# Engine programs in the main program instead of in a block, in a kernel of windowed attention and a gated spatial mixer

## The chip, the cores and the metric

One core of one Trainium2 chip runs the kernel. The metric is device time in microseconds (us). A run gives one such time. One further execution was taken by the hardware profiler; its span runs from the program's first recorded instruction to the end of its last.

## What is computed

`x` is 2048 rows of 512 values, bfloat16. It is normalised once, and two branches read the result; their sum and `x` are the output.

```python
xn = _layernorm(x)
# A: attention, 32 heads of 16, each row looks at 8 rows, 2 apart, up to itself
qkv = xn @ wqkv
logits = einsum('bhsd,bhswd->bhsw', q, kg) * scale     # kg, vg: gathered windows
o = einsum('bhsw,bhswd->bhsd', softmax(logits), vg)
# B: gated mixer, Fh = 896
z = gelu(xn @ w_in); z1 = z[..., :Fh]; z2 = _layernorm(z[..., Fh:])
g = einsum('ts,bsf->btf', w_sp, z2) + b_sp[None, :, None]
return x + o @ wo + (z1 * g) @ w_out
```

## The kernel before

The 2048 rows are 16 blocks of 128 (loops over `b`) and four groups of 512 (loops over `j` and `tc`). `ln_block` normalises a block on DVE, with the power on POOL (L561), and transposes it on PE (L573) or by DMA. `v_block` makes V (L598), which ACT evicts and POOL writes to a scratch tensor in DRAM (L606), from which SP later reads shifted windows (L846). `qk_pair` makes Q and K (L615), `prods` multiplies and adds windows on DVE (L636, L641), PE reduces over the head's 16 values (L649), `softmax` is DVE and ACT work. `z2_block` and `z1_group` make the two halves of z (L696, L740); `g_group` is the large product with `w_sp` (L823); `pv_block` weighs V by the attention on DVE (L851 to L857); `out_block` multiplies with `wo` (L879) and `w_out` (L888), DVE adds `x` (L894), and SP stores 128 rows (L899). The last block of rows is split by columns, and its second part is stored by ACT's queue.

None of this is issued where it is written. Every operation is a task in a `Plan`: an engine, a function that issues it, an estimated duration, what it reads and writes. `schedule` orders the tasks of each engine on a modelled clock. `emit` then goes over the engines in the order PE, ACT, DVE, POOL, SP and, for each, issues its tasks in its order; ahead of a task stand waits on semaphores (L310) for those tasks of other engines that it needs and that no earlier wait has covered. A DMA has a semaphore of its own channel.

The change touches how these five lists become programs. `build_kernel` opens `nc.Block()` (L391) within `with ExitStack() as es:` (L387). `emit` gets it as `block`, and `starters` (L283) maps an engine to `block.tensor`, `block.scalar`, `block.vector`, `block.gpsimd` or `block.sync`. Each of these opens a stretch of program for its engine, runs `body` in it, puts a jump into that stretch in the main program, and a jump to a common end behind it. When the `ExitStack` closes, the block writes the common end: each engine drains its own pipeline (DRAIN) and then meets the others: the engines count up a semaphore, POOL waits until all have, and then releases them all (EVENT_SEMAPHORE). The profile gives what the block adds at its end to L387.

What is written before that belongs to the launch (L952): small constants set by POOL, and a meeting of the same form, which every engine passes ahead of its first task.

The last thing in SP's list is `sp_final` (L927), the plan's final hook: it waits (L929) until the semaphores of all channels that write to DRAM, the scratch tensor's and the output's, have their full count.

Of the kernel before, what the change touches and what calls it, by code (L numbers as in the profile page):

```python
# [36 lines left out]
class Plan:  # L37
# [213 lines left out]
                                                                     last / 1000.0))  # L251


    def emit(self, nc, block, sems, chan_sems):
        for t in self.tasks:
            for d in t.deps:
                d.used = True
        cnt = {e: 0 for e in ENGS}
        for e in ENGS:
            for t in self.order[e]:  # L260
                if t.dma is None and t.used:
                    cnt[e] += 1
                    t.count = cnt[e]
                    t.tok = (("E", e), t.count)
        ccnt = {}
        for t in self.tasks:
            if t.dma is not None:
                c = t.dma["chan"]
                ccnt[c] = ccnt.get(c, 0) + 16
                t.count = ccnt[c]  # L270
                t.tok = (("C", c), t.count)
        self.chan_totals = dict(ccnt)
        for t in sorted(self.tasks, key=lambda x: (x.start, x.idx)):
            ck = {}
            for d in t.deps:
                for k, v in d.clock.items():
                    if ck.get(k, 0) < v:
                        ck[k] = v
            if t.tok is not None:
                ck[t.tok[0]] = max(ck.get(t.tok[0], 0), t.tok[1])  # L280
            t.clock = ck

        starters = {"pe": block.tensor, "act": block.scalar, "dve": block.vector, "pool": block.gpsimd,  # L283
                    "sp": block.sync}

        def semof(key):
            return sems[key[1]] if key[0] == "E" else chan_sems[key[1]]

        def run_engine(e):
            def body(eng):  # L290
                known = {}
                for t in self.order[e]:
                    need = {}
                    dl = [d for d in t.deps if known.get(d.tok[0], 0) < d.tok[1]]
                    for d in dl:
                        k, v = d.tok
                        implied = False
                        for d2 in dl:
                            if d2 is d:
                                continue  # L300
                            c2 = d2.clock.get(k, 0)
                            if c2 > v or (c2 == v and d2.tok != d.tok):
                                implied = True
                                break
                        if implied:
                            continue
                        if need.get(k, 0) < v:
                            need[k] = v
                    for k, v in need.items():
                        eng.wait_ge(semof(k), v)  # L310
                    for d in t.deps:
                        for k, v in d.clock.items():
                            if known.get(k, 0) < v:
                                known[k] = v
                    last = t.fn(eng)
                    assert last is not None, "task %s returned no instruction" % t.name
                    if t.dma is not None:
                        last.then_inc(chan_sems[t.dma["chan"]], 16)
                    elif t.used:
                        last.then_inc(sems[e], 1)  # L320
                fh = getattr(self, "final_hooks", {}).get(e)
                if fh:
                    fh(eng)
            starters[e](body)

        for e in ENGS:
            run_engine(e)


def build_kernel(nc, A_x, A_wqkv, A_wo, B_x, B_w_in, B_w_sp, B_b_sp, B_w_out, out, report=False, emit=True):  # L330
# [54 lines left out]
    plan = Plan()  # L385

    with ExitStack() as es:  # L387
        ar = es.enter_context(nc.sbuf_tensor("arena", [128, AR], BF))
        fp = es.enter_context(nc.sbuf_tensor("fpool", [128, FR], F32))
        ps = es.enter_context(nc.psum_tensor("ps", [128, PR], F32))  # L390
        block = es.enter_context(nc.Block())  # L391
        sem_h = {e: es.enter_context(nc.semaphore("sem_" + e)) for e in ENGS if e != "sp"}

        def A(name, n, o2_=0):
# [529 lines left out]
        chan_sems = {c: es.enter_context(nc.semaphore("c_%d" % i)) for i, c in enumerate(chans)}  # L924
# [4 lines left out]
                eng.wait_ge(chan_sems[c], plan.chan_totals[c])  # L929
        plan.final_hooks = {"sp": sp_final}  # L930
        with nc.allow_low_precision("bf16 intermediates by design"):
            plan.emit(nc, block, sem_h, chan_sems)
    return plan

def bass_parallel_sum__sliding_local_dilated__mixer_gmlp__prompt_kernel(
    nc, A_x, A_wqkv, A_wo, B_x, B_w_in, B_w_sp, B_b_sp, B_w_out, out
):
    build_kernel(nc, A_x, A_wqkv, A_wo, B_x, B_w_in, B_w_sp, B_b_sp, B_w_out, out)
# [28 lines left out]
```

## Time and profile before

| | |
|---|---|
| runs | 240.87, 241.27, 241.40 us; median 241.27 |
| the profiled execution's own time | 242.69 us |
| its span | 239.3 us (239.34 with one more digit); 3.35 us of its time lie outside |
| granted TensorE clock, mean | 0.999 |
| PE busy | 234.0 us, 98% of the span |
| DVE busy | 212.8 us, 89% |
| ACT, POOL busy | 98.1 and 33.2 us |
| PE rows on the chain that ended last | 69% of the span |

The span holds the launch's opening part and everything that the kernel writes, up to the last instruction of the block's common end. What the chip does before and after that in the measured time shows in no row. Lines with a "q" after the engine's name are of the engine's sequencer: waits, jumps, drains, issues of DMAs; they count for no busy time. In the answers about one line, the three numbers are the shortest, median and longest duration in nanoseconds, and behind them stand the starts of the first and the last one in us from the start of the span. A semaphore instruction that waits shows its whole wait as its duration on SP's queue in some rows (1965 ns for the longest at L929), and only its own few nanoseconds in others.

### The profile page before, as it was taken

What the parts mean: (1) busy time and instruction counts of PE and PEld (TensorE: products, weight loads), DVE (VectorE), ACT (ScalarE), POOL (GpSimd) and SP (SyncE); (2) the same over time, 40 slices, a digit from 0 to 9 for tenths busy, and PEclk for the clock granted to TensorE, in tenths of its full rate; (3) what the DMA queues carried; (4) which work ended last, traced back from release to release, by engine and by line L of the source; (5) the groups of instructions that cost most, each with busy time, mean ns of one, the idle gap of its engine ahead of it and who ended that gap; (6) DMA issues with size and microseconds to landing.
All of it is one profiled execution on the core that took longest, in us unless ns stands there. A gap on an engine that the chain in (4) does not pass through costs nothing.

```text
span 239.3 us, 3165 instructions
## 1 busy us (share of the span) xinstructions
PE 234.0 (98%) x1212; PEld 112.7 (47%) x1233; DVE 212.8 (89%) x267; ACT 98.1 (41%) x144; POOL 33.2 (14%) x56
## 2 busy tenths in 40 slices
PE   7999999999999999999999999999999999999995
PEld 3555555555444444444454444444444444444444
DVE  3798889999989899999999999986898999999952
ACT  2596889899888975541112111001010100101100
POOL 2378350401383500000000000000000000000000
PEclk9999999999999999999999999999999999999999
DMA  5997969993327110004079999999999997942112
GB/s 185 364 316 145 224 151 215 208 208 76 114 108 244 62 37 10 0 8 170 0 228 320 182 245 258 267 168 294 309 344 244 282 325 244 271 141 55 22 44 66
DMA packets 77806, 42.81 MB, mean 179 GB/s; under 512 B 50129, under 2 KB 77153, under 8 KB 77793
## 3 DMA queue, kind: packets, MB, share of 16 engines
q1 hardware_dynamic: 76480, 40.13, 66.2%
q0 software_dynamic: 800, 2.11, 2.8%
q10 hardware_dynamic: 512, 0.38, 0.5%
q8 instruction: 9, 0.15, 0.2%
q14 instruction: 5, 0.03, 0.1%
HBM read 26.35 MB, written 4.21 MB: 128 GB/s over the span
## 4 chain that ended last, share of the span: by engine, by line
PE 69%; DVE 16%; POOL 7%; issue 4%; POOLq 1%; ACT 1%; DVEq 0%
PE ps L823 40%; PE ps L888 10%; PE ps L879 6%; DVE arena L641 5%; PE ps L598 5%; DVE arena L636 4%; PE ps L615 3%; POOL fpool L723 3%; DVE arena L726 2%; PE ps L696 2%; POOL fpool L561 2%; PE ps L541 2%; POOL vscr L606 1%; POOLq L387 1%; DVE arena L563 1%
## 5 line engine op out<-in xcount | busy, mean ns | idle before, releaser
L823 PE MATMUL ps<-arena 128*128 128x512 bf16 x440 | 98.6, 379 | 0.4
L823 PEld LDWEIGHTS ps<-arena 128*128 128x128 bf16 x448 | 43.7, 98 | 52.6
L831 ACT ACTIVATE arena<-ps 128x1024 bf16<-128x1024 f32 (+1 forms) x16 | 14.7, 917 | 104.4 <-PE ps L823 93.8
L636 DVE TENSOR_TENSOR arena<-arena 128x4096 bf16<-128x4096 bf16 x16 | 36.6, 2285 | 0.2
L851 DVE TENSOR_TENSOR arena<-arena 128x4096 bf16<-128x4096 bf16 x16 | 36.5, 2284 | 0.0
L854 DVE TENSOR_TENSOR arena<-arena 128x2048 bf16<-128x2048 bf16 (+1 forms) x32 | 30.5, 953 | 0.4
L615 PE MATMUL ps<-arena 128*128 128x512 bf16 x126 | 28.5, 379 | 0.1
L641 DVE TENSOR_TENSOR arena<-arena 128x4096 bf16<-128x4096 bf16 x12 | 27.5, 2288 | 0.2
L888 PE MATMUL ps<-arena 128*128 128x512 bf16 (+2 forms) x116 | 26.8, 366 | 0.2
L696 PE MATMUL ps<-arena 128*128 128x448 bf16 x128 | 26.0, 352 | 0.0
L740 PE MATMUL ps<-arena 128*128 128x512 bf16 x109 | 24.2, 379 | 0.2
L615 PEld LDWEIGHTS ps<-arena 128*128 128x128 bf16 x128 | 14.5, 113 | 13.0
L894 DVE TENSOR_TENSOR arena<-ps,arena 128x512 bf16<-128x512 f32 (+2 forms) x17 | 11.2, 657 | 9.4 <-PE ps L888 9.4
L624 ACT ACTIVATE arena<-ps 128x1024 bf16<-128x1024 f32 x16 | 16.2, 1019 | 4.3 <-PE ps L615 3.6
L696 PEld LDWEIGHTS ps<-arena 128*128 128x128 bf16 x128 | 12.4, 98 | 11.5
L888 PEld LDWEIGHTS ps<-arena 128*128 128x128 bf16 x119 | 11.6, 98 | 12.7
L740 PEld LDWEIGHTS ps<-arena 128*128 128x128 bf16 x112 | 10.8, 98 | 12.7
L746 ACT ACTIVATE arena<-ps 128x1024 bf16<-128x1024 f32 (+1 forms) x16 | 14.1, 916 | 6.1 <-PE ps L740 6.1
L879 PE MATMUL ps<-arena 128*128 128x512 bf16 (+2 forms) x67 | 16.5, 366 | 0.1
L702 ACT ACTIVATE arena<-ps 128x896 bf16<-128x896 f32 x16 | 14.6, 913 | 2.8 <-PE ps L696 2.6
L598 PE MATMUL ps<-arena 128*128 128x512 bf16 x60 | 14.9, 379 | 0.4 <-ACT arena L579 0.2
L707 ACT ACTIVATE arena<-arena 128x896 bf16<-128x896 bf16 x16 | 15.2, 949 | 0.2
(56 smaller groups left out, 176.4 us busy)
## 6 DMA issues: line engine op xcount, KB each, us to landing
arena<-vscr SPq DMA_DIRECT2D x16, 1024.0 KB, 6.8
arena<-in_A_x_dram SPq DMA_DIRECT2D x29, 128.0 KB, 5.3
vscr<-arena POOLq DMA_DIRECT2D x16, 128.0 KB, 2.8
out_dram<-arena SPq DMA_DIRECT2D x15, 128.0 KB, 5.1
arena<-in_A_wqkv_dram SPq DMA_DIRECT2D x2, 512.0 KB, 6.6
arena<-in_B_w_in_dram SPq DMA_DIRECT2D x2, 448.0 KB, 5.2
arena<-in_B_w_in_dram SPq DMA_DIRECT2D x1, 896.0 KB, 5.3
arena<-in_B_w_out_dram SPq DMA_DIRECT2D x1, 896.0 KB, 5.5
```

The source lines that it names most:

```text
L598: last = t.matmul(P(bk, 512), AC(off["xnT"] + dc * S + 128 * b, [[1, 128]]), AC(off["wv"] + 512 * dc, [[1, 512]]), start=(dc == 0), stop=( ...
L615: last = t.matmul(P(bk, 512, 512 * which), AC(off["wqk"] + 2048 * which + 512 * dc + c, [[4, 128]]), AC(off["xnT"] + dc * S + 512 * j, [[1 ...
L624: T("act", lambda a: a.activation(AC(qo, [[ko - qo, 2], [1, 512]]), P(bk, 1024).rearrange("p (t n) -> p t n", t=2), ACTF.Copy, scale=0.5), ...
L636: T("dve", (lambda pbv, qb, kb: lambda v: v.tensor_tensor(pbv, qb, kb, ALU.mult))(pbv, qb, kb), reads=rd, writes=[("pb", s_)], est=c_tt(40 ...
L641: T("dve", (lambda av, bv: lambda v: v.tensor_tensor(av, av, bv, ALU.add))(av, bv), reads=[("pb", 1)], writes=[("pb", acc)], est=c_tt(4096 ...
L696: last = t.matmul(P(bk, 448, 512 * hf), AC(off["xnT"] + dc * S + 128 * b, [[1, 128]]), AC(off["w_in2"] + 896 * dc + 448 * hf, [[1, 448]]), ...
L740: last = t.matmul(P(bk, 512, 512 * i), AC(off["w_in1"] + 896 * dc + 128 * fc, [[1, 128]]), AC(off["xnT"] + dc * S + 512 * j, [[1, 512]]), ...
L823: last = t.matmul(P(bk, 512, 512 * i), AC(off["z2"] + FH * sh + 128 * fc, [[1, 128]]), AC(off["wT%d" % r_] + sh * 512, [[1, 512]]), start= ...
L851: T("dve", lambda v: v.tensor_tensor(tv, tv, av, ALU.mult), reads=[("attn", b)], writes=[("Vs", sv)], est=c_tt(4096), name="pv%d" % b, pri ...
L854: T("dve", (lambda n: lambda v: v.tensor_tensor(A("Vs", n, 4096 * sv), A("Vs", n, 4096 * sv), A("Vs", n, 4096 * sv + n), ALU.add))(n), wri ...
L879: last = t.matmul(P(bk, cn), AC(off["OT"] + 512 * tb + 128 * cc, [[1, 128]]), AC(off["wo"] + 512 * cc + c0, [[1, cn]]), start=(cc == 0), s ...
L888: last = t.matmul(P(bk, cn), AC(off["z1T"] + fc * S + 128 * tb, [[1, 128]]), AC(off["w_out"] + 512 * fc + c0, [[1, cn]]), start=False, sto ...
```

## The change

`emit` no longer takes a block. Each engine's `body` is called with the engine itself, so that its tasks, its waits and the final hook go into the main program, one engine's after the other's. `nc.Block()` is not opened. Thus the jumps into the engines' stretches, the jumps to the common end, the drains and the meeting at the end are not written. Tasks, their order, waits between them, buffers and DMAs are as before.

```diff
-    def emit(self, nc, block, sems, chan_sems):
+    def emit(self, nc, sems, chan_sems):
...
-        starters = {"pe": block.tensor, "act": block.scalar, "dve": block.vector, "pool": block.gpsimd,
-                    "sp": block.sync}
+        engines = {"pe": nc.tensor, "act": nc.scalar, "dve": nc.vector, "pool": nc.gpsimd, "sp": nc.sync}
...
-            starters[e](body)
+            body(engines[e])
...
-        block = es.enter_context(nc.Block())
...
-            plan.emit(nc, block, sem_h, chan_sems)
+            plan.emit(nc, sem_h, chan_sems)
```

## Prediction, made before the result was known

> **What bounds the kernel now.** I read the page's head first, then the shares of the chain of work that ended last.
>
> ```profile
> span 239.3 us, 3165 instructions
> ...
> PE 234.0 (98%) x1212; PEld 112.7 (47%) x1233; DVE 212.8 (89%) x267; ACT 98.1 (41%) x144; POOL 33.2 (14%) x56
> ...
> PE 69%; DVE 16%; POOL 7%; issue 4%; POOLq 1%; ACT 1%; DVEq 0%
> ```
>
> The reader is to see that the body is PE's, at 98% of the span, and that the rest of the chain is DVE, POOL and issue. The change edits no task, no order and no wait of this body. So the body can only be shifted as a whole, by what happens ahead of the first tasks; what else the change is worth lies behind the last store.
>
> Next I read the answers on the two lines that write sequencer instructions around the body: L952, the launch's opening, and L387, the block's end. First the opening; starts are in us.
>
> ```profile
> L952 SPq EVENT_SEMAPHORE  x1: 17/17/17, 0.7 to 0.7; - x1
> L952 ACTq EVENT_SEMAPHORE  x1: 17/17/17, 0.7 to 0.7; - x1
> L952 DVEq EVENT_SEMAPHORE  x1: 21/21/21, 0.7 to 0.7; - x1
> L952 PEldq EVENT_SEMAPHORE  x1: 51/51/51, 0.7 to 0.7; - x1
> ```
>
> ```profile
> L387 POOLq EVENT_SEMAPHORE  x2: 17/17/17, 239.2 to 239.2; - x2
> L387 POOLq DRAIN  x1: 4537/4537/4537, 80.1 to 80.1; - x1
> L387 PEldq DRAIN  x1: 512/512/512, 236.4 to 236.4; - x1
> L387 DVEq DRAIN  x1: 395/395/395, 236.7 to 236.7; - x1
> L387 ACTq DRAIN  x1: 153/153/153, 237.5 to 237.5; - x1
> L387 SPq COMPARE_BRANCH  x1: 41/41/41, 238.9 to 238.9; - x1
> L387 SPq DRAIN  x1: 13/13/13, 239.1 to 239.1; - x1
> L387 SPq EVENT_SEMAPHORE  x1: 17/17/17, 239.3 to 239.3; - x1
> ...
> L387 PEldq EVENT_SEMAPHORE  x1: 51/51/51, 239.3 to 239.3; - x1
> ```
>
> Two things are to be seen. Of the ten jumps in the source, five in and five out, only one is in the profile, on SP, at the end. And four engines have drained long before the end: POOL by 84.7, PE by 236.9, DVE by 237.1, ACT by 237.7 us. They wait for SP. What SP waits for is in the view of SP's own waits, and the last work in the timeline from 236.4 us on:
>
> ```profile
> SPq L929 <- DMA out_dram<-arena: 2.0, 1, 2.0
> ...
> SPq L387 <- PEq L387: 0.2, 1, 0.2
> ```
>
> ```profile
> 236.73 0.36 DVE L894 TENSOR_TENSOR arena<-ps,arena 128x192 bf16<-128x192 f32 x1 [0.41 <-PE ps L888]
> 237.12 0.36 ACTq L899 DMA_DIRECT2D out_dram<-arena  x1
> ```
>
> ACT issues the last store at 237.12; SP's wait for its landing ends at 238.69 (1.965 us from 236.725). That landing sets the end, and everything after it is SP alone.
>
> **The change part by part.** *SP's end.* After the landing the trace has, on SP: three more waits, starting at 238.737, 238.810 and 238.874, each 28 ns; the COMPARE_BRANCH at 238.941, 41 ns, which also carries SP's last wait (on a channel that landed long before); DRAIN at 239.119; POOL's two semaphore instructions at 239.157 and 239.235; the release on SP at 239.276, and on PE at 239.288 for 51 ns, which is the span's end, 239.339. After the change the last wait still has to be made, as a plain one in place of the branch: 238.941 + 0.028 = 238.969. All that comes later goes. So the span loses 239.339 - 238.969 = 0.37 us, and nothing is late next: the other engines' last rows end at 237.5 or before.
>
> *The drains* cost nothing now and nothing when gone: the one on POOL (4.5 us) lies beside 155 us of idle POOL, and those of PE, DVE and ACT end at least 1.0 us before the landing that SP waits for.
>
> *The jumps into the blocks.* The profile has no row for them. SP's first DMA issues at 0.797, 61 ns after its release from the opening meeting (0.719 + 0.017); between SP's waits at the end the gaps are 36 to 45 ns. The jump that did run was followed by 137 ns (238.982 to 239.119). A jump of that price does not fit into SP's 61 ns, so I take nothing; the upper bound for a hidden gain is 61 ns, were the whole gap the jump's, the lower bound zero, since the gap cannot fall below nothing. ACT's gap is 71 ns, POOL's 103, DVE's 172. POOL's and DVE's don't reach the end: their first tasks (memsets) feed warm-up matmuls and constants, while the first block's normalisation waits for x, whose DMAs SP and ACT issue.
>
> The Trainium skill prices these in "Advanced Engine Details and Errata", section "Control Flow Timing": about 51 ns for an unconditional branch and 108 ns for one that compares. The row at the end shows 41 ns and a gap, and no row shows an unconditional one; by the skill's figure the entry would give another 0.05 us and my time would be 0.05 us lower.
>
> *The part outside the span.* The profiled execution took 242.69 us, and 3.35 us of that lie outside the span, in no row. The engines must leave their programs there and, somehow, be known to have ended. The change can move this part both ways. At one end, the meeting that is removed is waited for again out there: +0.37 us, which gives back all. At the other, the four engines that are through at 237.7 do what they have to do after their programs under SP's wait: at most that wait's length, -1.97 us. Nearest to a small gain are the rows of the meeting itself: its steps from the last arrival on are 78 ns (239.157 to 239.235) and 41 ns (to 239.276), and a meeting to which all but SP have long come saves at most some such steps. I take -0.1 us, about one to two steps, and keep both ends.
>
> "Runtime: NRT & Kernel Launch", section "The ~15µs preamble/postamble breakdown", of the same skill speaks against the change: the runtime puts a barrier of its own, about 1.5 us, behind every kernel, which waits for all engines. No row here shows it. By it the kernel's own meeting is one of two, and what is saved is the first alone, 0.37 us; it gives no more.
>
> *Sum.* Against the profiled execution: 242.69 - 0.37 - 0.10 = 242.22 us, with a span of 238.97. That execution stands 1.42 us above the median of the runs; the same steps from the median give 241.27 - 0.47 = 240.80 us, 0.19% less.
>
> **The rivals.** *Moved, not saved.* The engines must be joined behind the kernel as well; if that join starts with the same drain and the same steps for SP, the span shows 0.37 us less and the part outside 0.37 us more: 241.27 us. For it: nothing in the span shows that the end of the program needs no join. Against: SP would have to pay a second time what it pays now, and the outside part would have to grow.
>
> *Much more than the span.* If the engines have work of their own after their programs, the removed meeting held it back until 239.3 for all of them. Then up to 1.97 us more goes; half of that, about 1.0, as the middle of an unknown, gives 241.27 - 0.37 - 1.0 = 239.9 us. For it: 3.35 us outside is nine times the meeting. Against: SP comes last either way, and its own part stays on the path.
>
> *Slower: an instruction fetch that is no longer covered.* The page has PE's programs coming by DMA:
>
> ```profile
> q8 instruction: 9, 0.15, 0.2%
> ```
>
> Nine transfers of 16 KB; their records last 0.88 to 1.33 us. Now none shows as a stall. The five programs are laid out anew, and where a piece of program begins relative to the 16 KB piece may shift. If one fetch comes to stand open on PE in the stretch from 101 to 236 us, where PE is busy 134.4 of 135 us, its whole 0.88 to 1.33 us reach the end: 240.80 + 0.88 to 240.80 + 1.33, 241.7 to 242.1 us. It decides from the point where more than 0.47 us of a fetch is uncovered, over 0.95 before a measurement can tell it. Against: the instructions between the opening and the last task are the same ones in the same number, and the removed ones are two or three per engine, at the end.
>
> *It does nothing at all*: the end is written in any case. Then no row at L387 would vanish and the time is 241.27; that is as good as excluded by the diff, and it goes with the first rival.
>
> **How the numbers follow.** This kernel's measurement can tell about 0.2%, 0.48 us, so faster begins below 240.79 and slower above 241.75. My forecast, 0.37 us of the span and little outside (240.6 to 241.0), gets 0.57; its point sits on the bound, so 0.32 of that is faster and 0.25 same. Moved, not saved: 0.12, same. Much more than the span: 0.18, faster. An open fetch: 0.11, taken as slower. The last 0.02 is same. That is 0.50 faster, 0.39 same, 0.11 slower. The predicted time is the forecast's, 240.80. The range has to leave out at most 0.2: it leaves the open fetch (0.11) and the lower half of the third case (0.09, below 239.9), so it goes from 239.9 to 241.6; the upper end takes in the case of no gain with the runs' own scatter of up to 0.4 us.
>
> **What would show it.** Right: no DRAIN, jump or semaphore row after SP's four waits at the end; SP's last wait ends near 238.97 and the span is 239.0; the first DMA issues again at 0.80 and the first PE matmul at 1.25; PE's busy time stays at 234.0; the execution's time less its span is 3.2 to 3.4 us. Moved, not saved: that difference rises to 3.7. Much more: it falls below 3.0. Open fetch: a gap on PE of about 1 us with no releaser. Entry jumps, if they did cost: the first DMA issues at 0.74 instead of 0.80. I am wrong at the root if the body itself changes length, by another order of tasks or other waits, since I took it as the same.

## The result, and the profile after

Over 22 executions each, the changed kernel took 240.41 us (239.94 to 242.48) and the kernel before 241.46 us (240.87 to 243.25). The ratio is 0.9965, with a 95% interval of 0.9950 to 0.9981: faster, by some 0.8 us and between 0.5 and 1.2. The medians stand 1.05 us apart, within that interval.

The page of the changed kernel's profiled execution (240.36 us), the lines that answer to those shown of before:

```profile
span 238.8 us, 3154 instructions
...
PE 233.8 (98%) x1212; PEld 112.6 (47%) x1233; DVE 212.8 (89%) x267; ACT 98.1 (41%) x144; POOL 33.2 (14%) x56
...
q8 instruction: 9, 0.15, 0.2%
...
PE 83%; DVE 12%; POOL 3%; issue 1%; ACT 0%; ACTq 0%
```

There are eleven instructions less in all. The engines' counts are the same, and their busy times agree to within 0.25 us. The chain's shares differ (PE 83% and POOL 3%, against 69% and 7%) with no task moved. Most likely the walk back took another of two near releasers in the first 100 us, where several engines lie close together; nothing is concluded from it.

The block's rows are gone from the trace. In their place, the last instructions are SP's waits, now at L927, and the opening (now L950) is as it was:

```profile
L927 SPq EVENT_SEMAPHORE  x5: 17/28/28, 238.5 to 238.8; - x5
```

```profile
L950 SPq EVENT_SEMAPHORE  x1: 17/17/17, 0.7 to 0.7; - x1
L950 ACTq EVENT_SEMAPHORE  x1: 17/17/17, 0.7 to 0.7; - x1
```

SP's first DMA issues at 0.799 us (0.797 before), the first matmul starts at 1.253 (1.251). So the entry gained nothing. At the end, the last store's issue and landing, from the timeline and from SP's waits:

```profile
236.59 0.36 DVE L892 TENSOR_TENSOR arena<-ps,arena 128x192 bf16<-128x192 f32 x1 [0.41 <-PE ps L886]
236.98 0.35 ACTq L897 DMA_DIRECT2D out_dram<-arena  x1
```

```profile
SPq L927 <- DMA out_dram<-arena: 2.0, 1, 2.0
```

The wait for the landing ends at 238.560, four more waits end at 238.832, and that is the span's end: 0.272 us behind the landing, where it was 0.649 (238.690 to 239.339). That is 0.377 us. The other 0.13 us by which this pair of spans differs (239.339 and 238.832, that is 0.507) came from the body, whose last store issued 0.14 us earlier. Bodies scatter: the changed kernel's spans went from 238.3 to 240.9 us. So spans are compared by their medians from here on.

What the single profiled execution of before could not tell is the part outside the span. Each execution of the comparisons has its own span, rounded to 0.1 us, and its own time; but for a few outliers, their difference scatters less than either. For the kernel before, in 31 executions taken together with the first experiments, the difference has a median of 2.22 us (28 of them between 2.16 and 2.26, then 2.34, 3.15 and 3.34). For the changed kernel it is 1.55 us (22 executions, 1.42 to 1.82 and one of 2.41). So 0.67 us went there, more than in the span, and the 3.35 us of the first profile were an exception (7 of 98 executions of before had 2.9 or more, counted over all comparisons of the next section).

### The profile page after: what moved, and what is told of

It reads as the page before. It is cut to its first block, busy times and chain, and to the rows that moved or that the text cites. A ratio compares the mean times of both kernels' runs of the same rounds, so it can differ in the third digit from the quotient of the medians.

```text
span 238.8 us, 3154 instructions
## 1 busy us (share of the span) xinstructions
PE 233.8 (98%) x1212; PEld 112.6 (47%) x1233; DVE 212.8 (89%) x267; ACT 98.1 (41%) x144; POOL 33.2 (14%) x56
## 4 chain that ended last, share of the span: by engine, by line
PE 83%; DVE 12%; POOL 3%; issue 1%; ACT 0%; ACTq 0%
PE ps L821 40%; PE ps L613 11%; PE ps L886 10%; PE ps L694 9%; PE ps L877 6%; DVE arena L639 4%; DVE arena L634 4%; PE ps L596 3%; POOL fpool L721 3%; PE ps L539 2%; DVE arena L724 2%; PE ps L647 1%; DVE arena L662 1%; DVE fpool L659 0%; PE ps L571 0%
```

## The experiments

The theory after the result: the removed meeting cost SP its 0.37 us in the span and held back all engines' ends, and letting these go early shortens the part outside by 0.67 us. The rivals: the jumps and the layout of the blocks cost something that no row shows; an instruction transfer for PE behind the span went (the trace of before has one of 16 KB at 241.70 us, 1.29 us long, the trace after has none there); what counts is SP's own drain and late release, not the others'.

All edits but that of the control are to the changed kernel. "Outside" is time less span; both it and the span are medians over the executions. The runs were made on three chips: e1 to e4, e5 to e8 and e9 to e12. Each ratio is to the kernel before on the same chip, whose part outside has medians of 2.22, 2.21 and 2.20 us there. On the chip of e5 to e8 no kernel ran with all engines let go early, so that the 1.55 us they are set against is from other chips.

| run | ratio to before, 95% interval | time, us | span, us | outside, us |
|---|---|---|---|---|
| before, with the first four | | 241.58 | 239.30 | 2.22 |
| changed (the result) | 0.9965 (0.9950 to 0.9981) | 240.41 | 238.90 | 1.55 |
| e1_before | 0.9998 (0.9982 to 1.0013) | 241.56 | 239.20 | 2.22 |
| e2_meeting | 1.0007 (0.9990 to 1.0024) | 241.77 | 239.45 | 2.21 |
| e3_pe_pad | 0.9951 (0.9929 to 0.9974) | 240.44 | 238.90 | 1.53 |
| e4_last_wait | 0.9938 (0.9913 to 0.9963) | 239.95 | 238.45 | 1.51 |
| e5_hold_all | 0.9979 (0.9969 to 0.9989) | 240.97 | 238.80 | 2.27 |
| e6_hold_pe | 0.9974 (0.9957 to 0.9992) | 240.76 | 238.95 | 1.78 |
| e7_hold_act | 0.9959 (0.9943 to 0.9975) | 240.54 | 238.80 | 1.73 |
| e8_hold_pool | 0.9976 (0.9962 to 0.9989) | 240.98 | 238.95 | 2.03 |
| e9_hold_dve | 0.9959 (0.9946 to 0.9973) | 240.52 | 239.00 | 1.55 |
| e10_act_waits | 0.9956 (0.9939 to 0.9974) | 240.39 | 238.70 | 1.67 |
| e11_pool_waits | 0.9958 (0.9940 to 0.9975) | 240.36 | 238.60 | 1.77 |
| e12_last_wait_again | 0.9949 (0.9930 to 0.9967) | 240.17 | 238.60 | 1.50 |

**The control, e1_before.** No edit.

> The kernel before, unchanged, to learn how much of its time lies outside the span from more than one execution. All theories: ratio 1.00 to within 0.2%, span near 239.4 us. Theory A (the removed meeting and drains are all there is): time less span is about 1.6 us in the usual execution, as in the 22 executions of the changed kernel (1.4 to 1.8, one of 2.4), so that the 3.35 us of the one profiled execution was an exception. Theory B (something behind the span got shorter too): it is 2.0 to 3.4 us in all of them.

Ratio 0.9998. Twelve executions had 2.15 to 2.37 us outside, and one of them 3.07. That settles it: 2.2 us is the rule for this kernel, theory B's lower end, and a reading near 3 us is a thing of single executions. The profiled one of this control had 2.20 us outside and no PE transfer behind its span, so that such a transfer is not what makes the 2.2 us.

**The meeting alone, e2_meeting.**

```diff
             plan.emit(nc, sem_h, chan_sems)
+            nc.all_engine_barrier()
```

> The changed kernel with one all-engine meeting, drains included, written behind the five programs; still no block and no jumps. Theory A: everything comes back, ratio to before 1.000, span as before (about 0.35 us more than changed). Rival J (the jumps and the layout of the blocks cost something that no row shows): the ratio stays near 0.998 or below, since the jumps are still gone.

Everything came back: ratio 1.0007, outside 2.21 us. The answer on the line that writes the meeting has the same rows as the block's end had, less the jump:

```profile
L931 POOLq EVENT_SEMAPHORE  x2: 17/17/17, 239.6 to 239.7; - x2
L931 POOLq DRAIN  x1: 4537/4537/4537, 80.6 to 80.6; - x1
L931 PEldq DRAIN  x1: 513/513/513, 236.9 to 236.9; - x1
L931 DVEq DRAIN  x1: 395/395/395, 237.3 to 237.3; - x1
L931 ACTq DRAIN  x1: 152/152/152, 238.0 to 238.0; - x1
L931 SPq DRAIN  x1: 13/13/13, 239.5 to 239.5; - x1
L931 SPq EVENT_SEMAPHORE  x1: 17/17/17, 239.7 to 239.7; - x1
```

So the blocks' jumps and layout, which are still absent here, were worth nothing that these ratios can tell (the interval is 0.17% to either side, 0.4 us), and the meeting with its drains brings back the saving within that. Its part of the span, from the end of SP's last wait (239.503) to PE's release (239.760), is 0.257 us. The block's end took 0.370, counted from 238.969, where a plain last wait would have ended; the 0.11 us between them are SP's jump with the gap behind it, which the trace shows and the ratio is too coarse to tell.

**PE's instruction transfer, e3_pe_pad.**

```diff
-        plan.final_hooks = {"sp": sp_final}
+        def pe_pad(eng):
+            for _ in range(8):
+                eng.drain()
+        plan.final_hooks = {"sp": sp_final, "pe": pe_pad}
```

> The changed kernel with eight DRAIN instructions more at the end of PE's program alone, after its last matmul, 1.8 us ahead of the landing that SP waits for. In the profile of before there is a tenth fetch of 16 KB for PE at 241.7 us, behind the span, 1.29 us long; the changed kernel has nine, and two PE instructions less. Theory F (that fetch is part of the saving): it comes back, time less span rises from 1.55 to 2 us or more, ratio to before about 0.998 to 1.000. Theory A: nothing changes against the changed kernel, ratio 0.9965, time less span 1.55 us.

Eight drains went onto PE's queue, and nothing moved: outside 1.53 us, ratio 0.9951, both those of the changed kernel.

```profile
L930 PEldq DRAIN  x8: 8/8/512, 238.7 to 239.6; - x8
```

(This execution's body was some 2 us longer than most; the medians are not touched by it.) No tenth transfer came, so that this run alone does not decide on theory F. Others do: the control has 2.20 us outside without the transfer, and the profiled execution of e9_hold_dve has a tenth one at 235.7 us, within the span, with 1.50 us outside. Theory F fell. The row here tells something more: these eight drains, which ended 1.3 us ahead of the landing on an engine that nobody waits for, cost nothing that the run can tell.

**Who is held back: e5_hold_all, e6_hold_pe, e7_hold_act, e8_hold_pool, e9_hold_dve.** The edit for all four; the other kernels name one engine.

```diff
             for c in dram_w_chans:
-                eng.wait_ge(chan_sems[c], plan.chan_totals[c])
+                last = eng.wait_ge(chan_sems[c], plan.chan_totals[c])
+            last.then_inc(sem_through, 1)
+        sem_through = es.enter_context(nc.semaphore("sem_through"))
         plan.final_hooks = {"sp": sp_final}
+        for e_ in ("pe", "act", "dve", "pool"):
+            plan.final_hooks[e_] = lambda eng: eng.wait_ge(sem_through, 1)
```

> The changed kernel; SP's last wait also counts up one new semaphore, and PE, ACT, DVE and POOL each wait for it as their last instruction. No drains, no block, and SP waits for nobody: SP's own end is where it was, the others end some 0.1 us behind it. So far, over all executions, time less span is 2.22 us with the meeting and 1.55 us without (median of 31 and of 22). Theory O (each engine has an ending of its own behind the program, which the meeting holds back and SP's wait now covers): time less span goes back to 2.1 to 2.25, the time to within 0.3 us of before, ratio about 0.9985 to 1.000. Theory S (what counts is SP's own drain and late release): 1.55 stays, ratio about 0.996.

> As the one that holds all four, but PE alone is held until SP is through. Theory O with PE's ending as the longest: time less span about 2.2. Theory O with another engine's: between 1.55 and 2.2. Theory S: 1.55.

> ACT alone is held until SP is through. Theory O: about 2.2 if ACT's ending is the longest, less if not; theory S: 1.55. ACT is the engine that ends second to last in the changed kernel (237.3 us), so that an ending of 0.65 us of it is covered by SP's wait with 0.8 us to spare.

> POOL alone is held until SP is through (in the changed kernel its last instruction ends at 83 us). Theory O: about 2.2 if POOL's ending is the longest, less if not; theory S: 1.55.

> DVE alone is held until SP is through. Medians of time less span so far: none held 1.55, ACT 1.73, PE 1.78, POOL 2.03, all four 2.27 us. Theory O (each engine has its own ending; the one that comes last with the longest ending sets the time): DVE's lies between 1.6 and 2.0. If the endings added up one after the other instead of lying beside each other, the four excesses over 1.55 (POOL 0.48, PE 0.23, ACT 0.18, DVE x) would sum to the 0.72 of all four, so x would have to be negative: time less span below 1.55.

With all four held, SP's five waits are as in the changed kernel, SP waits for nobody, and the others end within 0.08 us of it:

```profile
L927 SPq EVENT_SEMAPHORE  x5: 17/28/28, 238.6 to 238.9; - x5
```

```profile
L932 ACTq EVENT_SEMAPHORE  x1: 17/17/17, 238.9 to 238.9; - x1
L932 POOLq EVENT_SEMAPHORE  x1: 17/17/17, 238.9 to 238.9; - x1
L932 DVEq EVENT_SEMAPHORE  x1: 21/21/21, 238.9 to 238.9; - x1
L932 PEldq EVENT_SEMAPHORE  x1: 51/51/51, 238.9 to 238.9; - x1
```

The span stays short (median 238.80) and the part outside goes back to 2.27 us (four executions of ten had 1.93 to 1.99). That is near theory O's 2.1 to 2.25, and theory S, which wanted 1.55, fell: what the meeting did outside the span was to make the other engines late, not to make SP drain. The ratio, 0.9979, sits lower than the 0.9985 to 1.000 I expected; the span's 0.37 us are still saved here, and 0.37 of 241.4 us is 0.15%, so with its interval it fits a return of the outside part alone.

One engine at a time: POOL 2.03, PE 1.78, ACT 1.73, DVE 1.55 us. The ranges overlap with that of the changed kernel for PE (1.61 to 2.26) and ACT (1.49 to 1.86, of only five executions), so that ACT's share is the least sure; all ten of POOL lie at 1.97 or above. The row for POOL, which without the hold ends at 83 us:

```profile
L932 POOLq EVENT_SEMAPHORE  x1: 17/17/17, 238.9 to 238.9; - x1
```

So POOL's lateness costs most, 0.48 us, DVE's nothing. The held engine's own wait ends 0.04 to 0.08 us behind SP's; that lies in the span and comes on top. The excesses sum to 0.88 us (0.48, 0.23, 0.18 and -0.01), and all four together cost 0.72. They neither lie fully beside each other (that would be 0.48) nor fully one behind the other. Theory O in its simple form, in which the longest ending of a late engine sets the time, wanted 1.6 to 2.0 for DVE and missed; it also wants no more than POOL's 2.03 for all four, and their median is 2.27, though four of the ten executions lie below 2.0. That the engines' lateness costs is shown, what they do behind their programs is not.

**Another engine last: e10_act_waits and e11_pool_waits.** The order of the waits is that of e4_last_wait, shown below; only the engine that makes them differs.

```diff
-        plan.final_hooks = {"sp": sp_final}
+        plan.final_hooks = {"act": sp_final}
```

> The changed kernel with the order of final waits in which the store that lands last is waited for last, and these waits made by ACT, which issues that store, instead of SP; SP ends when its last store is issued, near 236.7 us. If each engine has an ending of its own length behind its program: the time less span is that of ACT's ending; if ACT's is shorter than SP's it falls below 1.55, with 1.4 the best I expect; if it is longer, up to 1.73. If SP's ending is needed by the others in turn, no difference: 1.5. Ratio to before 0.993 to 0.995.

> The same with the final waits made by POOL, which is otherwise through at 83 us. Theory O: POOL's ending is the longest of all, so time less span is about 2.0 although nobody meets anybody and all else is early; ratio to before about 0.9965. Rival (holding POOL cost something only since SP and POOL came late together): 1.5, ratio 0.994.

```profile
L927 ACTq EVENT_SEMAPHORE  x5: 17/38/1806, 237.4 to 237.7; - x5
```

```profile
L927 POOLq EVENT_SEMAPHORE  x5: 17/43/43, 237.6 to 238.3; - x5
```

The waits stand on ACT's queue in the first run (row above) and on POOL's in the second (row below it). With ACT last, and SP through near 236.1 us, outside is 1.67 us; with POOL last it is 1.77; with SP last, 1.50. So it does depend on which engine comes last, with nobody held by anybody. But POOL alone gives 1.77 and not the 2.03 that POOL with SP gave. Theory O's figure of 2.0 missed, and so did its rival's 1.5. That SP and POOL late together cost more than either alone is shown by these numbers (2.03 against 1.55 and 1.77; for ACT the like is 1.73 against 1.67, which is too close to tell); how the engines are joined behind the program is not, since no instruction's row lies there.

**A better end: e4_last_wait and e12_last_wait_again.**

```diff
-            for c in dram_w_chans:
+            for c in [("out", 4)] + [c for c in dram_w_chans if c != ("out", 4)]:
                 eng.wait_ge(chan_sems[c], plan.chan_totals[c])
```

The nine waits come out as five instructions, of which the first carries one wait and the others two each; the channel that is named first comes out in the last of them.

> The changed kernel with the same nine waits of SP at the end, in another order, so that the wait for the store that lands last stands in the last of the five instructions. Now four instructions stand behind that landing (238.543 to 238.832 us). If SP's path behind the last landing is what counts, the span falls by 0.27 us and the ratio to before goes from 0.9965 to about 0.9953. If the part outside the span does not follow SP, the span falls and time less span rises by as much: ratio unchanged.

> The order of the final waits in which the store that lands last is waited for last, on SP, once more, to compare with the one where ACT waits on the same chip and to see whether it is the best version. Expected as in its first run: span median 238.4 to 238.6 us, time less span 1.5, ratio to before 0.993 to 0.995.

```profile
L927 SPq EVENT_SEMAPHORE  x5: 17/28/462, 237.6 to 237.9; - x5
```

Four waits now start and end ahead of the landing (from 237.599 us on), and the fifth, started at 237.861, holds 462 ns until the landing and is the end of the span. Over the 14 executions of both, the median is 240.05 us, the span 238.55 and the part outside 1.50. Against the changed kernel and the one with padded PE together (34 executions: 240.43, 238.90, 1.55) that is 0.35 us off the span and 0.38 off the time; expected was 0.27. The trace accounts for that 0.27 alone (0.272 us behind the landing in the changed kernel, none here); the rest lies within the scatter of the bodies. The ratios, 0.9938 and 0.9949, lie below the changed kernel's 0.9965, and their intervals overlap with its own, so that the step is shown by the trace and the medians rather than by the ratio. It has the lowest median of this study.

## Why the prediction was right or wrong

The time, 240.41 us, lies in the range of 239.9 to 241.6, and the direction was right. The sum was not: it took 0.47 us off, and 1.05 came off by the medians (0.8 by the ratio), so that the time lies below the forecast's own 240.6 to 241.0. The range holds it because it kept the half of the second rival with the smaller gains, not because the sum was good.

*The body does not change*: right. Busy times and the start agree to within 0.25 us, the counts are the same, and the medians of span differ by 0.4 us (239.30 and 238.90), near the 0.37 of the end alone.

*SP's end, 0.37 us*: right. It measured 0.377 us from the landing on, and the medians agree within their scatter. (POOL's drain had ended by 84.62 us, not 84.7, which changes nothing.)

*The jumps into the blocks, nothing*: right. The first DMA issues at 0.799 us, and the meeting alone brings the time back to within 0.4 us either way. The Trainium skill's 51 ns for an unconditional branch ("Advanced Engine Details and Errata", "Control Flow Timing") would have made it 0.75, by an estimate from that figure; the measurement decides against it here, and no unconditional branch shows in any of these traces.

*The drains, nothing when gone*: right inside the span. Eight more of them on PE changed nothing that the run can tell.

*The part outside the span, -0.10 us*: the sum's wrong term, by its size. The step that failed was to price the outside by the steps of the meeting inside ("a meeting to which all but SP have long come saves at most some such steps"). It measured -0.67 us. In its place the runs showed what my second rival said, that the meeting held engines back until 239.3 and that their lateness costs behind the program: with all four held and no meeting, the part outside is 2.27 us again. I had priced that rival at 1.0 us and given it a chance of 0.18. What work the engines have there, which it assumed, no row shows. Put into the sum, 0.37 and 0.67 make 1.04 us; the medians of the result differ by 1.05.

Two things misled me. The 3.35 us outside, of one execution, looked like a large unknown; it was 2.2 in nearly all. So the signs I had named, 3.2 to 3.4 us for the forecast and below 3.0 for this rival, could not tell anything: the unchanged kernel lies below 3.0 too. What tells is the fall from 2.22 to 1.55. And I argued that "SP comes last either way", so its own part stays on the path. It does, and 1.5 us are left; but late POOL and PE, and less surely ACT, add to it.

On the skill's page "Runtime: NRT & Kernel Launch", section "The ~15µs preamble/postamble breakdown", I had set that the runtime's own barrier, about 1.5 us, waits for all engines, and concluded that no more than 0.37 us could be saved. The conclusion was wrong: without the kernel's meeting 1.05 us went by the medians, not 0.37. That the end waits for all engines agrees with the runs in which holding POOL, PE or ACT made the part outside longer; holding DVE, at 1.55 us, shows nothing of it. The page's three stages behind a kernel add up to 5 us by its figures, more than the 1.5 to 2.2 us that lie outside here, so the measured time cannot hold all of them at these lengths.

*Moved, not saved*: wrong; the part outside shrank instead of growing. *An open instruction fetch*: did not come; PE has nine transfers in the span in both, and from 101 to 236 us it is busy 134.37 us in both. *It does nothing at all*: excluded; all rows of the block's end are gone.

## What to carry to other kernels

In this kernel a meeting of all engines at the end cost twice: the steps behind the last landing, which the trace shows, and the late end of the engines that were through, which only time less span shows. So it is worth a try to let each engine end when it is done, and to let one engine wait for the outputs. Among the waits at the end, put the one that ends last into the last instruction. When an edit lies at an edge of the program, compare time less span over many executions: 28 of 31 of the kernel before lie between 2.16 and 2.26 us, and 21 of 22 of the changed one between 1.42 and 1.82, while their spans range over 2.6 us and more. Take medians, since single executions can lie 1 us off.

## What the runs showed that I had not expected

Which engine ends last changes the time outside the span: 1.50 us with SP, 1.67 with ACT, 1.77 with POOL; 1.78 with SP and PE late together, 2.03 with SP and POOL, 2.27 with all five. Why SP and POOL late together cost more than one of them stays open; a trace with instructions' rows behind the span would be needed. One record does lie there in every profile, a transfer of 8 KB on the second instruction queue (q14). It begins 1.03 to 1.05 us behind the span's end with the meeting (before, e1, e2) and 1.30 to 1.35 without it and with nobody held (after, e3, e4, e12). So between these two groups it comes later where the part outside is shorter; what it is for, and whether anything waits for it, no run shows.
